# Attention with hashed buckets into a gated feed-forward layer: one pair of heads is loaded, turned around and hashed in another way

## The chip, the cores and the metric

The kernel runs on one core of a Trainium2 chip. The metric is the device time of one execution in microseconds (us). The time before is a median of 336.03 us over three runs, from 335.37 to 336.10 us.

## The reference, cut to what matters

There are 4 batches of 8 heads, 768 positions and 64 features a head. A query may attend to a key only if both fall into the same bucket of 64, found by the signs of six projections.

```python
q_bits = (einsum('bhsd,dk->bhsk', q, proj) > 0)      # proj: 64 x 6
k_bits = (einsum('bhsd,dk->bhsk', k, proj) > 0)
mask   = q_bucket[..., :, None] == k_bucket[..., None, :]
scores = where(mask, q @ k.T / sqrt(64), -1e9)
attn   = softmax(scores)                              # + 1e-9 in the sum
x      = (attn @ v) as rows of 3072 x 512             # heads side by side
xn     = x / sqrt(mean(x * x) + 1e-6) * rms_g         # the norm
out    = (silu(xn @ w_gate) * (xn @ w_val)) @ w_out   # 512 -> 1536 -> 512
```

## The kernel before, in words

**Units, heads and steps.** The work is cut into eight units: unit `u` is half `u % 2` of the queries of batch `u // 2`, 384 queries by eight heads. A head of a unit is three steps, each of which makes the scores of 256 keys by 384 queries (two matmuls, `scores`, L322) and their exponentials (one ScalarE instruction, `probs`, L334). There are 192 such steps, 24 for a unit. The order of heads is (unit 0, heads 0 and 1), (unit 1, heads 0 and 1), then the rest of unit 0, the rest of unit 1, and units 2 to 7. Unit 0 thus ends its scores with step 29, and unit 2, the first of batch 1, begins with step 48.

**The plan.** At every step the program issues the scores of the next step, the exponentials of this one, and then all that is listed in `plan[t]`, in the order in which `at(0, t, ...)` entered it. Engines and DMA queues run their instructions in this order, so a list entry that waits holds back whatever comes behind it on its engine. The last thing of a head is `av` (L347), attention times V, in two parts; `attn_out` (L361 to L373) scales its result into `x` and squares it, and `sumsq` (L377) sums the squares.

**Pairs of heads.** Keys and queries of two heads come together, as the pair `(b, hp)`. A pair is loaded on SyncE's DMA queue (`load_natural`, L94, or `load_blocks`, L117, the latter in runs of 128 bytes), turned so that features lie on partitions, copied into the operand tile `QK` in 16 bits, and hashed: the six sign bits of each position become six more rows of `QK`, so that equal buckets give the highest score. Six pairs, all of batch 0 and the first two of batch 1, are turned by TensorE: `turn_pe` transposes three blocks of one head into a PSUM bank (L149), and VectorE copies it out (L151). These pairs are hashed by `hash_pairs` (L223: eight matmuls into two banks, on 64 rows each), `signs` (L212) twice, and `send` (L262: four DMAs of 9.0 KB). The ten other pairs are turned by VectorE and hashed by `hash_one` (L203: four matmuls into one bank, on 128 rows; `signs` once; L282: eight DMAs of 4.5 KB).

**The end of unit 0.** The steps around the change are 20 to 48. Unit 0's last head has its `av` in steps 30 and 31. In step 31 VectorE runs the last `attn_out` of the unit and the sums, GpSimd the power that gives `rstd` (L393); then `norm` multiplies two thirds of `x` (VectorE, L404), and in step 37 (`TX`) ScalarE the last third. Then `turn_x` transposes the normed rows (L411) into `xnT`. From step 38 on the first unit's `gate` and `value` matmuls (L428) are laid between the scores of unit 1 by `spread`, which holds a table of weights for each kind of work (`HASH` is 1000) and puts the hashes of `inserts` ahead of the first gate at or behind their step. The weights of the feed-forward layer come on GpSimd's DMA queue (`load_w`, L523), as six DMAs from step 22 on.

Of the kernel before, what the change touches and what calls it, by code (L numbers as in the profile page):

```python
# [8 lines left out]
FP32 = mybir.dt.float32  # L9
# [9 lines left out]
D = 64  # L19
# [3 lines left out]
HALF = 384  # L23
# [10 lines left out]
def kernel(  # L34
# [12 lines left out]
    nc = tc.nc  # L47
# [3 lines left out]
    lpool = ctx.enter_context(tc.tile_pool(name="lpool", bufs=8))  # L51
# [13 lines left out]
    ident = const.tile([128, 128], FP32, name="ident")  # L65
# [15 lines left out]
    def bank(name, shape=None, dt=FP32):  # L81
        return gps.tile(shape or [128, 512], dt, name=name, tag="g")


    raw = {}

    def load_natural(eng, b, hp, which, heads=(0, 1)):
# [10 lines left out]
            ),  # L98
        )

    def load_v(eng, b, hp):
        vn = lpool.tile([128, 2, 6, D], FP32, name="vn", tag="L")
        eng.dma_start(
            out=vn.rearrange("p h c d -> p h (c d)"),
            in_=v[b, 2 * hp : 2 * hp + 2].rearrange("h (p c) d -> p h (c d)", c=6),
        )
        raw[b, hp][2] = vn
# [18 lines left out]


    PARITY = (0, 1)
    ONPE = [(0, hp) for hp in range(4)] + [(1, 0), (1, 1)]
    KROWS = D + 6  # L130
    qT, kT, QK = {}, {}, {}

# [8 lines left out]
    def turn_pe(b, hp, hh, which, keep=nc.vector.tensor_copy, act=(), ps=None):  # L141

        src = raw[b, hp][0 if which == "q" else 1][:, hh].rearrange(
            "p (j e) d -> p j (e d)", e=2
        )
        if ps is None:
            ps = bank("t_ps", [128, 3, 128])
        for j in range(3):
            nc.tensor.transpose(ps[:, j, :], src[:, j], ident)  # L149
        psf = ps.rearrange("p j t -> p (j t)")  # L150
        keep(turned(b, hp, which)[:, hh, :], psf)  # L151
        o = 0 if which == "q" else S
        for e in act:
            nc.scalar.copy(
                QK[b, 2 * hp + hh, "h"][0:64, o + e * HALF : o + (e + 1) * HALF],
                psf[64 * e : 64 * e + 64, :],
            )

    def turned(b, hp, which):
        return (qT if which == "q" else kT)[b, hp].rearrange("p (h c) -> p h c", h=2)  # L160
# [26 lines left out]
    def cast_pool(b, hp, which):  # L187
        if (b, hp) in ONPE:
            for e in range(2):
                cast_part(b, hp, which, e)  # L190
            return
        src = (qT if which == "q" else kT)[b, hp]
        o = 0 if which == "q" else S
        for hh in range(2):
            nc.gpsimd.tensor_copy(  # L195
                QK[b, 2 * hp + hh, "h"][0:64, o : o + S], src[64 * hh : 64 * hh + 64, :]
            )
# [295 lines left out]
    load_natural(nc.sync, 0, 1, "k")  # L493
    load_natural(nc.sync, 0, 1, "q")
    load_v(nc.sync, 0, 0)
    load_v(nc.sync, 0, 1)
    load_natural(nc.sync, 0, 2, "k")
    load_natural(nc.sync, 0, 2, "q")
# [37 lines left out]
    def at(w, s, f, *a):  # L536
        plan[NS * w + s].append(lambda: f(*a))

    new_pair(0, 0)
    turn_pe(0, 0, 0, "k", act=(0,))  # L540
    spare = [
        scps.tile([128, 2, 512], FP32, name="s_ps")[:, 0, 0:HALF].rearrange("p (j t) -> p j t", j=3)
        for _ in range(2)
    ]
    turn_pe(0, 0, 0, "q", act=(0,), ps=spare[0])
    cast_part(0, 0, "k", 1, 0, 1)
    turn_pe(0, 0, 1, "k", ps=spare[1])
    idle(1)
    _, direct, _, _ = hash_direct(0, 0, (0,))
# [55 lines left out]
    at(0, 1, load_natural, nc.sync, 0, 3, "k")  # L605
    at(0, 1, load_natural, nc.sync, 0, 3, "q")
    at(0, 2, load_v, nc.sync, 0, 2)
    at(0, 2, load_v, nc.sync, 0, 3)
    at(0, 6, v_prep, 0, 1)
    at(0, 15, v_prep, 0, 2)  # L610
    at(0, 19, v_prep, 0, 3, nc.vector)
    for hp, t in enumerate((4, 16, 21, 31)):
        at(0, t, v_mean, 0, hp, 2, range(6))
    for i, t in enumerate((22, 34)):
        cols = slice(i * DFF // 2, (i + 1) * DFF // 2)
        at(0, t, load_w, wg, moe_w_gate, 0, 4, cols)
        at(0, t + 3, load_w, wv, moe_w_val, 0, 4, cols)
        at(0, 39 + 3 * i, load_w, wo, moe_w_out, 6 * i, 6)


    for hp, ts in ((0, (8, 22, 23, 24, 25, 24, 26, 26, 28, 42)), (1, (20, 27, 28, 29, 30, 29, 41, 32, 33, 43))):
        tl, ts = ts[0], ts[1:]
        for w in "kq":
            at(0, tl, load_natural, nc.sync, 1, hp, w)
        at(0, tl, load_v, nc.sync, 1, hp)
        at(0, ts[0], new_pair, 1, hp)
        for t, hh, w in zip(ts[0:4], (0, 1, 0, 1), "kkqq"):
            at(0, t, turn_pe, 1, hp, hh, w)
        at(0, ts[4], cast_pool, 1, hp, "k")
        at(0, ts[5], cast_pool, 1, hp, "q")  # L630
        if hp == 0:
            at(0, ts[6], hash_pair, 1, hp)
            at(0, ts[7], send_pair, 1, hp)
        at(0, ts[8], v_prep, 1, hp)
        at(0, ts[8], v_sum, 1, hp)

    spots = {
# [11 lines left out]
    TX = 37  # L649
# [9 lines left out]
    for n, (u, h) in enumerate(order):  # L659
        t = 3 * n + 4 - ((u, h) == (0, H - 1))  # L660
        for part in range(2):
            at(0, t + part, av, u, h, part)
        if h % 2:
            if (u, h) == (0, H - 1):

                at(0, t + 1, o_step, u, h // 2, nc.vector)
                at(0, t + 1, s_step, u, h // 2)
                at(0, t + 1, norm_scale, u)
                at(0, t + 2, hash_only, 1, 1)
                at(0, t + 2, hash_signs, 1, 1)  # L670
                at(0, t + 2, norm, u)
                at(0, TX, norm_third, u, 2, nc.scalar.mul)
                at(0, TX + 1, send_pair, 1, 1)
                at(0, TX - 1, idle, 2, bank)
                at(0, TX, idle, 1, bank)
                for c in range(3):
                    at(0, TX, turn_x, u, c, c == 2)
                continue
            at(0, t + 1, o_step, u, h // 2)
            at(0, t + (6 if h < 7 else 3), s_step, u, h // 2)  # L680
# [36 lines left out]
    for u in range(7):  # L717
# [11 lines left out]
        for i in range(9):  # L729
            c, n = divmod(i, 3)  # L730
# [12 lines left out]
    def behind_norm(t):  # L743

        return t - t % NS + 7 if 1 <= t % NS < 7 else t

    for (b, hp), (load, kturns, qturns, _) in spots.items():
        at(0, load, load_blocks, nc.sync, b, hp)
        at(0, load, load_v, nc.sync, b, hp)
        at(0, kturns[0], new_pair, b, hp)  # L750
        for w, turns in (("k", kturns), ("q", qturns)):
            for i, t in enumerate(turns):
                at(0, t, turn_dve, b, hp, w, i, len(turns))
            at(0, behind_norm(turns[-1] + 1), cast_pool, b, hp, w)
        t = behind_norm(qturns[-1] + 2)
        at(0, t, v_prep, b, hp)
        at(0, t, v_sum, b, hp)
# [64 lines left out]
```

## Time and profile before

| what | value |
|---|---|
| three runs | 335.37, 336.03, 336.10 us |
| profiled execution | 335.25 us, of which the traced span is 333.4 us |
| TensorE matmul | 325.7 us busy, 3004 instructions |
| VectorE | 238.0 us busy, 487 instructions |
| ScalarE | 225.3 us busy, 327 instructions |
| GpSimd | 152.9 us busy, 205 instructions |
| SyncE's DMA queue | 75528 packets, 25.45 MB |
| GpSimd's DMA queue | 3680 packets, 4.72 MB |

The page of the profile lists busy time by engine, the chain of work that ended last, and groups of instructions by line with their mean duration. The chain and the order of instructions can also be asked for any stretch of the span, in microseconds from its start, and so can the packets that the DMA queues moved in it.

### The profile page before, as it was taken

To read this page: it belongs to the slowest core of one execution; us is meant where nothing else is said; L and a number is where in the kernel's file an instruction comes from. 1 tells how busy PE (TensorE), PEld (TensorE's weight loads), DVE (VectorE), ACT (ScalarE), POOL (GpSimd) and SP (SyncE) were. 2 spreads that over 40 slices of the span, in tenths; PEclk is the share of its full clock that TensorE was granted. 3 is DMA by queue.
4 is the path that set the end of the run, shared out by engine and by line. 5 is a ranking of instruction groups with operands and counts; after the bars stand their busy time and mean duration, and the time that the engine had idled before them with its cause. 6 is when DMAs were issued, how large, how long until landed. Compare 5 with 4: busy or idle time off the path is not lost.

```text
span 333.4 us, 7810 instructions
## 1 busy us (share of the span) xinstructions
PE 325.7 (98%) x3004; PEld 196.8 (59%) x3004; DVE 238.0 (71%) x487; ACT 225.3 (68%) x327; POOL 152.9 (46%) x205
## 2 busy tenths in 40 slices
PE   7999989999999999999999999999999999999996
PEld 3576656655565565655566565655656566664554
DVE  3887877778878668876888568886776456674870
ACT  3899886676677667676767667776676857754322
POOL 3698859229724743726483622656371111122000
DMA  7941999978129545341807036001000010002002
GB/s 216 349 151 42 252 166 209 204 131 189 68 41 161 96 131 107 51 98 67 168 16 142 11 102 131 7 3 67 34 4 2 4 62 33 0 2 84 14 0 94
DMA packets 79692, 30.92 MB, mean 93 GB/s; under 512 B 64988, under 2 KB 76712, under 8 KB 79656
## 3 DMA queue, kind: packets, MB, share of 16 engines
q1 hardware_dynamic: 75528, 25.45, 32.4%
q0 software_dynamic: 3680, 4.72, 8.4%
q8 instruction: 23, 0.38, 0.5%
q10 hardware_dynamic: 448, 0.27, 0.3%
q14 instruction: 13, 0.11, 0.1%
HBM read 28.32 MB, written 6.29 MB: 104 GB/s over the span
## 4 chain that ended last, share of the span: by engine, by line
PE 86%; DVE 5%; DMA 3%; SPq 1%; POOL 1%; ACT 1%; issue 1%; ACTq 0%; DVEq 0%; POOLq 0%
PE v_ps L428 18%; PE g_ps L428 17%; PE s_ps L322 17%; PE y_ps L457 16%; PE o_ps L347 10%; PE d_ps L203 2%; PE t_ps L149 2%; PE x_ps L411 2%; PE d_ps L223 2%; DMA qL<-in_q_dram 2%; SPq L282 1%; DMA pj<-in_proj_dram 1%; DVE xn L404 1%; ACT psb L334 1%; PE y_ps L476 1%
## 5 line engine op out<-in xcount | busy, mean ns | idle before, releaser
L334 ACT ACTIVATE psb<-s_ps,ebias 128x768 f16<-128x768 f32 x192 | 167.9, 900 | 21.8 <-PE s_ps L322 20.8
L322 PE MATMUL s_ps<-QK 70*128 70x384 f16 x384 | 93.6, 326 | 1.9 <-ACT psb L334 1.5
L436 ACT ACTIVATE t<-g_ps 128x384 f32<-128x384 f32 x96 | 47.2, 492 | 54.5 <-PE g_ps L428 54.3
L428 PE MATMUL g_ps<-xnT,wg 128*128 128x384 f16 x384 | 82.6, 325 | 0.1
L428 PE MATMUL v_ps<-xnT,wv 128*128 128x384 f16 x384 | 81.7, 325 | 0.2 <-DVE a L445 0.2
L445 DVE SCALAR_TENSOR_TENSOR a<-t,g_ps 128x384 f32<-128x384 f32 x96 | 52.8, 550 | 27.5 <-ACT t L436 25.9
L368 POOL TENSOR_TENSOR x<-otmp,rcp 128x384 f32<-128x384 f32 x31 | 25.9, 837 | 96.0 <-DVE rcp L366 95.5
L457 PE MATMUL y_ps<-wo,ht 128*128 128x512 f16 x276 | 68.0, 378 | 0.0
L347 PEld LDWEIGHTS <-psb 128*128 128x128 f16 x1152 | 52.0, 97 | 16.0 <-issue 1.2
L446 DVE SCALAR_TENSOR_TENSOR ht<-a,v_ps 128x384 f16<-128x384 f32 x96 | 53.2, 554 | 11.4 <-PE v_ps L428 3.2
L347 PE MATMUL o_ps<-vl,psb 128*128 128x65 f16 x1152 | 56.3, 193 | 0.0
L322 PEld LDWEIGHTS <-QK 70*128 70x128 f16 x384 | 34.6, 98 | 35.6 <-issue 12.7
L428 PEld LDWEIGHTS <-wv 128*128 128x128 f16 x384 | 35.2, 97 | 22.3 <-issue 1.4
L428 PEld LDWEIGHTS <-wg 128*128 128x128 f16 x384 | 34.7, 97 | 21.1 <-DVE xnT L417 0.6
L457 PEld LDWEIGHTS <-ht 128*128 128x128 f16 x276 | 24.6, 97 | 22.6
L373 POOL TENSOR_TENSOR sq<-x 128x384 f32<-128x384 f32 x31 | 25.7, 827 | 2.4
L469 ACT COPY ysb<-y_ps 128x512 f32<-128x512 f32 x23 | 13.5, 586 | 19.6 <-PE y_ps L457 19.6
L195 POOL CAST QK<-qT 64x768 f16<-64x768 f32 x20 | 16.6, 832 | 19.0 <-DVE qT L182 17.0
L361 DVE TENSOR_TENSOR otmp<-o_ps,cvb 128x390 f32<-128x390 f32 x32 | 17.8, 557 | 8.7 <-PE o_ps L347 8.5
L377 DVE TENSOR_REDUCE ssp<-sq 128x3 f32<-128x384 f32 x32 | 16.9, 529 | 9.9 <-POOL sq L373 9.7
L195 POOL CAST QK<-kT 64x768 f16<-64x768 f32 x20 | 16.5, 826 | 12.6 <-PE s_ps L322 7.3
L404 DVE TENSOR_SCALAR xn<-x,rstd 128x512 f16<-128x512 f32 x23 | 16.1, 754 | 7.2 <-POOL rstd L393 7.2
(79 smaller groups left out, 263.6 us busy)
## 6 DMA issues: line engine op xcount, KB each, us to landing
vn<-in_v_dram SPq DMA_DIRECT2D x16, 384.0 KB
out_dram<-ysb SPq DMA_DIRECT2D x23, 256.0 KB
qL<-in_q_dram SPq DMA_DIRECT2D x40, 96.0 KB
kL<-in_k_dram SPq DMA_DIRECT2D x40, 96.0 KB
kn<-in_k_dram SPq DMA_DIRECT2D x5, 384.0 KB
qn<-in_q_dram SPq DMA_DIRECT2D x5, 384.0 KB
wg<-in_moe_w_gate_dram POOLq DMA_DIRECT2D x2, 768.0 KB, 8.2
wv<-in_moe_w_val_dram POOLq DMA_DIRECT2D x2, 768.0 KB, 10.4
```

The source lines that it names most:

```text
L195: nc.gpsimd.tensor_copy(QK[b, 2 * hp + hh, "h"][0:64, o : o + S], src[64 * hh : 64 * hh + 64, :])
L322: nc.tensor.matmul(ps[:, j, 0:HALF], QK[b, h, "h"][0:KROWS, S + jt * 128 : S + (jt + 1) * 128], QK[b, h, "h"][0:KROWS, half * HALF : (half ...
L334: nc.scalar.activation(psb[u, h][:, 2 * ch : 2 * ch + 2, :], sps.pop((u, i))[:, :, 0:HALF], AF.Exp, bias=ebias, scale=ESCALE,)
L347: nc.tensor.matmul(o[:, c, hh, 0:65], psb[u, h][:, jt, c * 128 : (c + 1) * 128], vls[b % 2][:, h, 2 * (jt % 3) + jt // 3 if b in PARITY el ...
L368: eng.tensor_mul(xd.rearrange("p c (h d) -> p c h d", h=2), tmp[:, :, :, 0:64], r.to_broadcast([128, 3, 2, 64]),)
L373: eng.tensor_mul(sq, xd, xd)
L404: mul(xn[u][:, c, :], x[u][:, c, :], rstds[u][:, c : c + 1])
L428: nc.tensor.matmul(ps, w[:, kt, fs], xnT[u][:, kt, :], start=(kt == 0), stop=(kt == 3))
L436: nc.scalar.activation(t, fbank[u, ft, "g_ps"], AF.Tanh, scale=0.5)
L445: nc.vector.scalar_tensor_tensor(out=a, in0=t, scalar=1.0, in1=g, op0=ALU.add, op1=ALU.mult)
L446: nc.vector.scalar_tensor_tensor(out=ht[u][:, ft, :], in0=a, scalar=0.5, in1=vv, op0=ALU.mult, op1=ALU.mult)
L457: nc.tensor.matmul(y, ht[u][:, ft, c * 128 : (c + 1) * 128], wo[:, ft, :], start=(ft == 0), stop=(ft == NF - 1),)
```

## The change

Of the second pair of batch 1, `(1, 1)`, both tiles are now loaded by `load_mixed`, which lays the two heads side by side for every position: four DMAs instead of two, in runs of 64 numbers (256 bytes) instead of 384. A transposed block then holds both heads' features on 128 partitions, so that the pair can be hashed as `hash_one` does it. It is still turned by TensorE, twelve blocks by three (`turn_mixed`): the keys in steps 28 and 30 (four turns in steps 27 to 30 before), the queries in steps 32 and 33, between the sums of unit 0's norm and its multiplications. The hash in step 32 and its four sends in step 38 go; `hash_one` comes among unit 0's gates at step 42. The three matmuls on zeros in steps 36 and 37 are dropped. Some steps move: `v_mean` of pair (0, 3) from 31 to 29, the first weight loads from 22 and 25 to 21 and 24, the queries' cast of pair (1, 0) from 26 to 31, the casts of pair (1, 1) from 29 and 41 to 38 and 39.

```diff
+    def load_mixed(eng, b, hp):
+        tiles = []
+        for name, t in (("kn", k), ("qn", q)):
+            lt = lpool.tile([128, 6, 2, D], FP32, name=name, tag="L")
+            for hh in range(2):
+                eng.dma_start(
+                    out=lt[:, :, hh], in_=t[b, 2 * hp + hh].rearrange("(p c) d -> p c d", c=6)
+                )
+            tiles.append(lt)
+        raw[b, hp] = tiles[::-1] + [None]
...
-    ONPE = [(0, hp) for hp in range(4)] + [(1, 0), (1, 1)]
+    ONPE = [(0, hp) for hp in range(4)] + [(1, 0)]
...
+    def turn_mixed(b, hp, which, e, keep):
+        src = raw[b, hp][0 if which == "q" else 1]
+        ps = bank("t_ps", [128, 3, 128])
+        for j in range(3):
+            nc.tensor.transpose(
+                ps[:, j, :], src[:, 2 * j + e].rearrange("p h d -> p (h d)"), ident
+            )
+        dst = (qT if which == "q" else kT)[b, hp][:, e * HALF : (e + 1) * HALF]
+        keep(dst, ps.rearrange("p j t -> p (j t)"))
...
-    for hp, t in enumerate((4, 16, 21, 31)):
+    for hp, t in enumerate((4, 16, 21, 29)):
         at(0, t, v_mean, 0, hp, 2, range(6))
-    for i, t in enumerate((22, 34)):
+    for i, t in enumerate((21, 34)):
...
+    at(0, 31, cast_pool, 1, 0, "q")
...
+    at(0, 20, load_mixed, nc.sync, 1, 1)
+    at(0, 20, load_v, nc.sync, 1, 1)
+    at(0, 28, new_pair, 1, 1)
+    for e, t in enumerate((28, 30)):
+        at(0, t, turn_mixed, 1, 1, "k", e, nc.vector.tensor_copy)
+    at(0, 38, cast_pool, 1, 1, "k")
+    at(0, 39, cast_pool, 1, 1, "q")
...
     spots = {
+        (1, 1): (None, None, None, 42),
...
-                at(0, t + 2, hash_only, 1, 1)
-                at(0, t + 2, hash_signs, 1, 1)
-                at(0, t + 2, norm, u)
+                at(0, t + 2, turn_mixed, 1, 1, "q", 0, nc.vector.tensor_copy)
+                at(0, t + 3, turn_mixed, 1, 1, "q", 1, nc.vector.tensor_copy)
+                at(0, t + 3, norm, u)
                 at(0, TX, norm_third, u, 2, nc.scalar.mul)
-                at(0, TX + 1, send_pair, 1, 1)
-                at(0, TX - 1, idle, 2, bank)
-                at(0, TX, idle, 1, bank)
```

More of the change, by code (lines that the diff above doesn't have):

```diff
@@ L618 @@
         at(0, 39 + 3 * i, load_w, wo, moe_w_out, 6 * i, 6)
[L621 to L635, printed above, removed]
+    for w in "kq":
+        at(0, 8, load_natural, nc.sync, 1, 0, w)
+    at(0, 8, load_v, nc.sync, 1, 0)
+    at(0, 22, new_pair, 1, 0)
+    for t, hh, w in zip((22, 23, 24, 25), (0, 1, 0, 1), "kkqq"):
+        at(0, t, turn_pe, 1, 0, hh, w)
+    at(0, 24, cast_pool, 1, 0, "k")
+    at(0, 31, cast_pool, 1, 0, "q")
+    at(0, 26, hash_pair, 1, 0)
+    at(0, 28, send_pair, 1, 0)
+    at(0, 42, v_prep, 1, 0)
+    at(0, 42, v_sum, 1, 0)
+    at(0, 20, load_mixed, nc.sync, 1, 1)
[5 more added lines that the diff above has]
+    at(0, 39, cast_pool, 1, 1, "q")
+    at(0, 43, v_prep, 1, 1)
+    at(0, 43, v_sum, 1, 1)
     spots = {
[1 row of a table added]
         (1, 2): (34, (48, 48), (49, 49), 51),
@@ L747 @@
     for (b, hp), (load, kturns, qturns, _) in spots.items():
+        if load is None:
+            continue
         at(0, load, load_blocks, nc.sync, b, hp)
```

## The prediction

> **What bounds the kernel now.** I read the page first, then the chain of waits around the change in order of time, then the DMA queues by stretch, then SyncE's queue. The page:
>
> ```profile
> PE 325.7 (98%) x3004; PEld 196.8 (59%) x3004; DVE 238.0 (71%) x487; ACT 225.3 (68%) x327; POOL 152.9 (46%) x205
> ...
> PE 86%; DVE 5%; DMA 3%; SPq 1%; POOL 1%; ACT 1%; issue 1%; ACTq 0%; DVEq 0%; POOLq 0%
> ```
>
> TensorE carries 86% of the chain, so a matmul added there is paid, and so is any wait of TensorE, which runs in order. The exception matters here. The chain from 35 to 47 us (start, duration, what):
>
> ```profile
> 38.81 0.33 PE s_ps L322 x2
> 39.14 0.37 PE m_ps L307 x6
> ...
> 40.20 0.57 DVE otmp L361
> ...
> 42.81 0.18 DVE ss L389
> ...
> 43.04 0.44 issue
> 43.48 0.91 POOL rstd L393
> ...
> 44.41 1.05 DVE xn L404 x2
> ...
> 45.51 0.62 PE x_ps L411 x8
> ```
>
> From 39.5 to 45.5 us unit 0's norm is the bound. TensorE only keeps ScalarE's exponentials fed; in the chain its next pieces are the transposes, and the first gate starts at 47.00 us. So the hash (40.02 to 40.9 us) and the zeros (43.4 to 44.6 us) that the change takes away lie beside the norm.
>
> The DMA queues, each row giving packets, MB and share of 16 engines. First 32.5 to 35.4 us, where pair (1, 1) lands in packets of 1536 bytes:
>
> ```profile
> q1 hardware_dynamic: 711, 1.04, 99.4%
> ```
>
> Then 36 to 42 us, the weights (q0) over SyncE's queue (q1):
>
> ```profile
> q0 software_dynamic: 765, 1.15, 110.8%
> q1 hardware_dynamic: 43, 0.04, 2.5%
> ```
>
> Then 47 to 54 us, where pair (1, 2) in 128-byte packets meets more weights:
>
> ```profile
> q0 software_dynamic: 867, 1.31, 106.9%
> q1 hardware_dynamic: 864, 0.11, 19.8%
> ```
>
> Weights move at about 127 packets a us whether alone or in company; SyncE's queue, with both waiting, gets one packet for each of theirs, however small. Last, SyncE's queue, behind pair (1, 2):
>
> ```profile
> 62.29 2.95 SPq L262 DMA_DIRECT2D QK<-bits  x4
> 65.34 0.64 SPq L117 DMA_DIRECT2D qL<-in_q_dram  x1
> ```
>
> It issues without a pause worth the name from 62 to 86.5 us, about 0.7 us a DMA.
>
> **The change part by part.**
>
> *The norm starts earlier.* Steps 27 to 31 lose two turns before unit 0's last `av` (each three transposes, 0.33 us in the chain: 0.66 us); the limit becomes the exponentials, 0.79 us apart. Counting scores, turns, `v_mean` and `av` through, the last `av` ends near 39.3 us instead of 39.77, VectorE no longer has the `cvb` of `v_mean` (0.29 us) in front of `otmp`, and GpSimd, rid of 1.72 us of casts ahead of `x` and `sq`, gives the earlier sums sooner. `otmp` starts at 39.35 instead of 40.20: gain 0.85 us. Exponential 37, which ScalarE's third of the norm follows, goes from 43.73 to 42.95. By itself this brings the first gate to about 46.2: a gain of 0.8 us. The 0.44 us ahead of `rstd` occurs once (for later units the power starts 0.08 us after the sum ends), while the hash's two `signs` run on VectorE; if they cause it, up to 0.4 us more. I take none, since `rstd`'s first use explains it as well.
>
> *Turns, signs, zeros.* Twelve transposes and four copies stay. One `signs` (0.55 us of VectorE) goes. Zeros: 3 x 0.22 us at their pace, where TensorE waits anyway: nothing. The queries' two copies (1.1 us) sit between the sum and `xn` on VectorE, beside the power's 0.91 us plus the wait before it, as the two `signs` did: nothing, if the queries are there.
>
> *The hash among the gates.* Four matmuls on 128 rows are 0.78 us in the chain (eight on 64 rows 0.88), now in a stretch that is TensorE without a gap (15.00 busy of 47 to 62 us): +0.78 us. Its copy of signs hides beside VectorE's 11.04 of those 15 us.
>
> *The load.* This decides. Before, the pair comes as 512 packets; now as 2 x 1536 of 256 bytes. One costs, on the line between 128 bytes (12.9 ns, from 2084 packets at 84.2% in 67 to 69 us) and 1536 bytes (64.9 ns, from the row above), about 17.6 ns: 909 a us, an estimate from rows. Issues start at 30.88 us as before, packets flow at about 32.5. The weights' first DMA is issued from 32.07 to 33.08 us; one step earlier in the plan changes nothing, since GpSimd has no work between the two places. The next DMA passes the casts of the keys, and follows at 33.9 instead of 35.99: no gap in the weights. Before, their first packet came at 35.4, 2.3 us after the issue, when the 1536-byte ones ran out; a later one (issue ending at 45.2) took 0.75 us, small packets ahead. The 1.6 us between are some 25 packets of 65 ns already queued. With 17.6 ns ones that is 0.45 us, so the weights join at about 34.3. By then (34.3 - 32.5) x 909 = 1640 packets are through: the keys, in time for their turn at 35.8, and 100 of the queries. The other 1430 are 90 to an engine. The weights' 1024 are 64 to an engine and take 8.0 us; meanwhile the queries get 64, the remaining 26 take 0.5 us: landed at 42.8, seen by TensorE at about 43.2. If the weights join at 35.4 as before, 27 to an engine are left, and the queries are seen at 39.2. If each packet costs the 25.7 ns of the mixed stretch from the start, 44.2. I take 43.2: the short queue ahead is the nearer case.
>
> *Who waits.* The queries' turn in step 32 is due at 39.45. Behind it on TensorE stand the scores of step 34 on, so ScalarE runs dry at 40.7. With queries at 43.2: exponential 34 at 44.1, then 0.79 us each, 37 at 46.45; ScalarE's third ends at 48.0 instead of 45.26, the transposes about 48.4 instead of 46.13, first gate 49.2 instead of 47.00: +2.2 us. `xn` on VectorE waits behind both copies, to 45.7: earlier than ScalarE's third. The sum is 2.2 + 0.78 = +3.0 us. Each us of the queries' arrival moves the gates by one: at 39.2 they come 0.8 earlier (sum 0), at 41.5 they come 0.5 later (+1.3), at 44.2 they come 3.2 later (+4.0).
>
> *SyncE's queue.* Eight sends for four add 4 x 0.70 = 2.8 us behind 62.3 us. The loads behind them are wanted 3 us later or more. The tight one is pair (1, 2)'s hash: its sends start at 80.71, the second lands at 83.7, and the scores that need it start at 85.02. A 2.8 us shift less up to 0.9 us of pauses makes them 0.6 to 1.5 us late, unless TensorE is itself 3 us later: nothing in my main case, a rival otherwise. The first read of the moved hash is step 53, at 73.2: the eight sends end near 68. Casts of (1, 1) on GpSimd, at steps 38 and 39, come after `rstd`, and nobody needs them before step 48: nothing.
>
> The profiled execution took 335.25 us (span 333.4, 1.85 around it), 0.78 under the median. Its sum is 338.2; I add the 3.0 to the median: 339.0 us, own range 337.3 to 340.0 (the +1.3 and +4.0).
>
> **The rivals.**
>
> *The queries come in time and nothing else is late (not slower).* It holds if they are seen by about 40.3 us, when TensorE's wait just eats the gain of 0.8. For it: the weights' first packet waited until SyncE's queue was drained. Against it: the equal counts of 47 to 54 us. Then -0.8 + 0.78, less up to 0.4 for `rstd` and up to all of the hash if it fits a gap: 334.8 to 336.0, likeliest 335.6.
>
> *In time, but the sends are late.* Then 0.6 to 1.5 us at step 59, less up to 0.4: 336.3 to 337.5. For it: 1.3 us of slack against 2.8. Against it: pauses in the queue.
>
> *The clock falls.* The first eight zeros in this trace, at 1.2 to 4.1 us, took up to 634 ns, those at 43 us 377 to 380. A TensorE idle from 39.8 to 43.2, with no zeros behind, could lose that state, though the windows grant 1.00 throughout and no idle stretch after the start is over 0.76 us. Half pace for some 4 us, in a stretch where TensorE has 0.6 of each 0.79 us step, costs about 1.7 us more: 340.7. The Trainium skill (TensorE: Matmul & The Clock Gate, What's actually happening) states half the clock after an idle window of about 3.4 us; no run here shows it in mid-kernel.
>
> *The load is no different* (the program merges its runs) can't be: each head's 64 numbers lie between the other's.
>
> **How the numbers follow.** Late queries 0.52, clock 0.10, late sends 0.13, in time 0.25. Late queries and the clock are slower; of late sends 0.10 is slower by over 0.2% (0.67 us, about what a measurement of this kernel can tell from no change), 0.03 within; of in time 0.13 is faster by that, 0.12 within. Slower 0.72, same 0.15, faster 0.13. The range leaves out the better half of the faster cases and the worst of the clock: 335.2 to 340.6.
>
> **What would show it.** Right: 256-byte packets on SyncE's queue one for one with the weights from about 34 to 42 us; the first transposes of `turn_mixed` that read `qn` beginning near 43 us, with TensorE idle before it and ScalarE idle after exponential 33; first gate near 49; four `d_ps` of `hash_one` (0.78 us) more; 88 sends of 4.5 KB for 80. Wrong: queries turned by 39.5 us, a first gate at or before 46.5, or an idle TensorE ahead of the scores at 85 us instead.

## The result

The changed kernel takes 343.81 us (median of four runs, 343.51 to 345.84) against 335.96 us for the kernel before in the same comparison: a ratio of 1.0242 with a 95% interval of 1.0213 to 1.0270. That is 7.9 us slower. The prediction had the direction and the mechanism, but only 3.0 us of it, and the time lies outside its range.

The page of the changed kernel: busy time by engine, the granted TensorE clock in 40 slices of the span, and the chain that ended last.

```profile
PE 327.8 (96%) x2993; PEld 198.2 (58%) x2993; DVE 236.8 (69%) x486; ACT 225.4 (66%) x327; POOL 152.8 (45%) x205
...
PEclk9999969999999999999999999999999999999999
...
PE 82%; DMA 8%; DVE 5%; SPq 1%; ACT 1%; POOL 1%; issue 1%; ACTq 0%; POOLq 0%; DVEq 0%
```

TensorE has fewer instructions than before and more busy time, and one slice shows a lower clock: some matmuls ran slowly. DMA has gone from 3% of the chain to 8%. The chain in order of time names the transfer (start, duration, what):

```profile
33.12 13.29 DMA qn<-in_q_dram
46.42 0.14 issue
46.55 0.87 PE t_ps L176 x3
47.42 0.64 PE s_ps L345 x2
...
52.21 0.62 ACT xn L427
...
54.14 0.68 PE g_ps L451 x4
```

The queries' turn (L176) was due at 40.2 us, behind the scores of step 33, and starts at 46.55. Three transposes then take 0.87 us where 0.33 was the rule, and two score matmuls 0.64 instead of 0.33: half pace. The first gate starts at 54.14 us against 47.00 before. TensorE and the clock by stretch (length, then busy time of PE, PEld, DVE, ACT and POOL, then the granted clock, DMA share and GB/s):

```profile
40.00:43.00 3.00, 0.33 (x3) 0.00 (x0) 2.69 (x7) 1.46 (x2) 0.73 (x1) 1.00 1.16 201
43.00:50.00 7.00, 3.45 (x21) 2.60 (x22) 1.81 (x4) 1.52 (x2) 4.14 (x5) 0.53 1.19 229
```

TensorE had 0.33 us of work from 40 to 43 us. From about 43 us the clock is halved, while it is still idle; it comes back at 50.

The packets, first in 32 to 34 us (SyncE's queue alone, q1):

```profile
q1 hardware_dynamic: 1227, 0.31, 68.1%
```

Then 34 to 36 us, where the weights (q0) join:

```profile
q0 software_dynamic: 116, 0.18, 87.6%
q1 hardware_dynamic: 381, 0.09, 22.6%
```

And 36 to 43 us:

```profile
q0 software_dynamic: 788, 1.19, 93.0%
q1 hardware_dynamic: 752, 0.19, 20.7%
```

Alone, 1227 packets, nearly all of 256 bytes, take 68.1% of 2 us on 16 engines, 17.8 ns each. From 36 us on it is one for one, 752 to 788, and the queries crawl at 107 packets a us.

### The profile page after: what moved, and what is told of

It reads as the page before. It is cut to its first block, busy times and chain, and to the rows that moved or that the text cites. A ratio compares the mean times of both kernels' runs of the same rounds, so it can differ in the third digit from the quotient of the medians.

```text
span 341.8 us, 7795 instructions
## 1 busy us (share of the span) xinstructions
PE 327.8 (96%) x2993; PEld 198.2 (58%) x2993; DVE 236.8 (69%) x486; ACT 225.4 (66%) x327; POOL 152.8 (45%) x205
## 4 chain that ended last, share of the span: by engine, by line
PE 82%; DMA 8%; DVE 5%; SPq 1%; ACT 1%; POOL 1%; issue 1%; ACTq 0%; POOLq 0%; DVEq 0%
PE v_ps L451 17%; PE g_ps L451 17%; PE s_ps L345 16%; PE y_ps L480 15%; PE o_ps L370 9%; DMA qn<-in_q_dram 4%; PE d_ps L226 2%; PE x_ps L434 1%; SPq L305 1%; PE d_ps L246 1%; PE t_ps L161 1%; DMA pj<-in_proj_dram 1%; ACT psb L357 1%; DVE xn L427 1%; DMA kL<-in_k_dram 1%; PE y_ps L499 1%
## 5 line engine op out<-in xcount | busy, mean ns | idle before, releaser
L345 PE MATMUL s_ps<-QK 70*128 70x384 f16 x384 | 94.6, 329 | 2.1 <-ACT psb L357 1.6
L370 PEld LDWEIGHTS <-psb 128*128 128x128 f16 x1152 | 52.4, 97 | 16.8 <-issue 2.1
L218 POOL CAST QK<-qT 64x768 f16<-64x768 f32 x22 | 18.3, 830 | 19.0 <-DVE qT L205 17.0
L218 POOL CAST QK<-kT 64x768 f16<-64x768 f32 x22 | 18.2, 826 | 13.0 <-PE s_ps L345 7.6
```

The costliest lines, as they stand in the source:

```text
L218: nc.gpsimd.tensor_copy(QK[b, 2 * hp + hh, "h"][0:64, o : o + S], src[64 * hh : 64 * hh + 64, :])
L345: nc.tensor.matmul(ps[:, j, 0:HALF], QK[b, h, "h"][0:KROWS, S + jt * 128 : S + (jt + 1) * 128], QK[b, h, "h"][0:KROWS, half * HALF : (half ...
L370: nc.tensor.matmul(o[:, c, hh, 0:65], psb[u, h][:, jt, c * 128 : (c + 1) * 128], vls[b % 2][:, h, 2 * (jt % 3) + jt // 3 if b in PARITY el ...
```

## The experiments

**Small packets alone.** The kernel before, with nothing but the load cut:

```diff
+        if (b, hp) == (1, 1):
+            for e in range(2):
+                src = (q, k)[i][b, 2 * hp : 2 * hp + 2].rearrange("h (p j e) d -> e p h j d", e=2, j=3)
+                dst = raw[b, hp][i].rearrange("p h (j e) d -> e p h j d", e=2)
+                for hh in range(2):
+                    eng.dma_start(out=dst[e][:, hh], in_=src[e][:, hh])
+            return
```

> The kernel before, with only the key and query loads of pair (1, 1) cut into runs of 256 bytes (four DMAs a tensor, the same 3072 packets as in the change, layout, turns and hash as before). Theory: the load alone does it; the queries' turn, due at 37.1 us, waits to about 46 us and the norm behind it too: first gate 53 to 56 us, time 342.5 to 345.5 us. Rival (the load is harmless, the moved work costs the time): 335.5 to 336.7 us.

Measured: 347.08 us, ratio 1.0337 (1.0312 to 1.0362). That is 11.2 us, more than the whole change and more than I expected. TensorE's rows, with its wait and what ended it in brackets ("issue" where the profile shows nothing):

```profile
40.05 0.88 PE L156 MATMUL t_ps<-ident,kn 128*128 128x128 f32 x3 [4.23 <-issue]
...
43.54 0.87 PE L156 MATMUL t_ps<-ident,kn 128*128 128x128 f32 x3 [1.97 <-issue]
...
46.61 0.87 PE L156 MATMUL t_ps<-ident,qn 128*128 128x128 f32 x3 [1.07 <-DMA qn<-in_q_dram]
```

So the small packets alone, with the weights' DMAs in their old places, make TensorE wait, and the queries come at the same 46.6 us. But this is not the change's load. It has four DMAs for each tensor where the change has two, and issues them until 39.8 us, where the change is done at 33.8. From 32 to 35 us SyncE's queue moved 805 packets, against 1559 in the changed kernel, and the keys alone are 1536. So here the keys were most probably late too: of the 7.3 us of waiting, 6.2 stand ahead of the keys' turns. All these turns stand ahead of unit 0's last head and of its norm, and the clock is halved from 38.7 to 52.4 us. The 11.2 us are thus no price of the change's load, and whether turning the queries inside the norm made that load cheaper isn't shown.

**Zeros in the wait.** The changed kernel with one line more:

```diff
+                at(0, t + 2, idle, 28, bank)
                 at(0, t + 2, turn_mixed, 1, 1, "q", 0, nc.vector.tensor_copy)
```

> The changed kernel with 28 matmuls on zeros (128x512, 0.215 us each, 6.0 us) ahead of the queries' turn in step 32, so that TensorE is busy while it would wait. Theory (the wait costs some 5.5 us and the lost clock some 1.7 us on top): clock 1.00 throughout, the turn still starts at 46 to 46.6 us but at full pace, first gate at 52.2 to 52.8 us, time 341.7 to 342.5 us. Rival (the slow clock costs nothing, since ScalarE's exponentials set the pace there): 343.4 to 344.2 us.

Measured: 342.30 us (342.06 to 342.52), 1.5 us less than the changed kernel; clock 1.00. Its TensorE in order of time:

```profile
40.06 6.21 PE L541 MATMUL z_ps<-zeros 128*128 128x512 f16 x28
47.02 0.52 PE L176 MATMUL t_ps<-ident,qn 128*128 128x128 f32 x3 [0.76 <-DMA qn<-in_q_dram]
```

and its first gate in the chain:

```profile
53.12 0.68 PE g_ps L451 x4
```

The turn comes 0.47 us later than in the changed kernel, the gate 1.0 us earlier. So the lost clock costs some 1.5 us, and the wait is there whatever TensorE does meanwhile.

**Weights later.** The changed kernel with its first two weight loads at steps 25 and 26:

```diff
-    for i, t in enumerate((21, 34)):
+    for i, t in enumerate((25, 34)):
...
-        at(0, t + 3, load_w, wv, moe_w_val, 0, 4, cols)
+        at(0, t + (1 if i == 0 else 3), load_w, wv, moe_w_val, 0, 4, cols)
```

> The changed kernel with the first two weight loads at steps 25 and 26 instead of 21 and 24, nothing else. Theory (the 256-byte packets share the engines one for one with the weights, so the queries come 6 us late, and the idle TensorE loses its clock on top): the weights' first packets come at about 36 us, when pair (1, 1) is through; the queries' turn starts by 40.2 us, no TensorE idle over 1 us, clock 1.00, first gate at 46.3 to 47.5 us, time 335.5 to 337.5 us. Rival (the hash among the gates, the turns inside the norm and the eight sends cost the time): 341 us or more, with the queries early.

Measured: 341.21 us, ratio 1.0154 (1.0124 to 1.0183): only 2.6 us better. Half of the expectation held. The queries' turn starts at 40.50 us, no idle TensorE, clock 1.00, first gate near 47.1. The time of the profiled execution went into two other waits. In its chain, the second weights now come late:

```profile
36.51 12.18 DMA wv<-in_moe_w_val_dram
48.69 0.05 issue
48.74 0.82 PE v_ps L451 x4
```

And at step 60, in TensorE's timeline, the scores wait for the bits of pair (1, 2):

```profile
89.44 0.48 PE L345 MATMUL s_ps<-QK 70*128 70x384 f16 x2 [2.12 <-DMA QK<-bits]
```

That is the rival of the late sends, at a higher price than its 0.6 to 1.5 us. In the changed kernel it stays hidden, since TensorE is 8 us late by then. The profiled execution, at 339.90 us with a clock of 1.00, is the fastest of the four; the others took 341.18 to 342.10 with a mean clock of 0.995. Some of their time is thus probably clock lost in such a wait, which no trace shows.

**Load earlier.** The whole mixed load at step 17:

```diff
-    at(0, 20, load_mixed, nc.sync, 1, 1)
+    at(0, 17, load_mixed, nc.sync, 1, 1)
```

> The changed kernel with the mixed load at step 17 instead of 20 (V stays at 20), ahead of the sends of pair (0, 3). Theory (the packets only have to be through before the weights start at 34 us): issues from about 25.7 to 28.3 us, landed by 31 us, the queries' turn starts by 40.2 us, clock 1.00; the sends of pair (0, 3) go out some 0.3 us later, which the scores of step 24 see; time 335.5 to 337.5 us. Rival (it is the moved hash and turns): 341 us or more.

Measured: 337.59 us, ratio 1.0057 (1.0037 to 1.0078). With the same packets, ahead of the weights, 6.2 us are back. The turn starts at 42.15 us without waiting for its data. What is left shows in the chain: the sends of pair (0, 3), now behind the load, come late for step 24.

```profile
30.36 3.10 DMA QK<-bits
33.60 0.48 PE s_ps L345 x2
```

**Queries early, keys in place.** To spare those sends, only the queries are loaded at step 17:

```diff
+    at(0, 17, load_mixed, nc.sync, 1, 1, "q")
+    at(0, 20, load_mixed, nc.sync, 1, 1, "k")
```

> The changed kernel with the mixed queries loaded at step 17 and the mixed keys at step 20, so that neither runs into the weights and the sends of pair (0, 3) aren't held up. Theory (with the load in time, what is left are the hash among the gates, +0.6 us, and pair (1, 2)'s sends behind four more DMAs, seen as a TensorE wait at the scores of step 60, 2.3 us in the run with later weights): no wait at steps 24 and 34, first gate within 0.5 us of 47 us, a wait of 1.3 to 2.5 us at step 60, 337.0 to 338.5 us. Rival (the sends cost nothing and only the load matters): 335.5 to 336.5 us, no wait at step 60.

Measured: 337.34 us, ratio 1.0042 (1.0025 to 1.0059). The time is as expected, for another reason in the profiled execution. It shows no wait at step 60; instead the keys came late for step 28:

```profile
32.24 5.96 DMA kn<-in_k_dram
38.20 0.14 issue
38.34 0.52 PE t_ps L174 x3
```

That execution ran 0.6 us late from its start, and its last keys fell among the weights. The run with the zeros, below, ran 0.4 us late and had its keys in time, so what decided it isn't known, nor how often it happens in the unprofiled executions.

**Sends ahead of loads.** In addition the load of pair (2, 0) moves behind the hash of (1, 2):

```diff
-        (2, 0): (50, (63, 64, 65, 66), (67, 69, 70, 71), 73),
+        (2, 0): (52, (63, 64, 65, 66), (67, 69, 70, 71), 73),
```

> As the run before, and the load of pair (2, 0) at step 52 instead of 50, so that pair (1, 2)'s eight sends go ahead of its nine DMAs. Theory: the wait at step 60 goes, 1.3 to 2.5 us less than the run before, 335.5 to 336.7 us; equal to the kernel before within its uncertainty, since the norm's earlier start and the hash among the gates cancel. Rival (the wait at step 60 has another cause): as the run before.

Measured: 336.18 us, ratio 1.0014 (0.9998 to 1.0029): equal to the kernel before, 1.2 us less than the run ahead of it. SyncE's queue shows the new order, the sends from 75.62 us, then the load:

```profile
75.62 5.78 SPq L303 DMA_DIRECT2D QK<-bits  x8
81.50 2.71 SPq L127 DMA_DIRECT2D qL<-in_q_dram  x4
```

No TensorE wait for data is left in its profile between 24 and 100 us, neither for the keys nor for the bits. I can't divide the 1.2 us between the two, since the run ahead had the keys' wait in its profile. First gate in the chain:

```profile
46.33 0.68 PE g_ps L449 x4
```

**With the zeros.** The same with the three matmuls on zeros back.

```diff
+                at(0, TX - 1, idle, 2, bank)
+                at(0, TX, idle, 1, bank)
```

> As the run before, with the three matmuls on zeros of steps 36 and 37 back. Theory: TensorE waits there anyway, and without a wait of several us it keeps its clock with or without them: the same within 0.2 us. Rival (the zeros hold the clock up): 1 us or more faster, and the run before shows a stretch at half clock.

Measured: 336.30 us, ratio 1.0018 (0.9999 to 1.0036), the same as without them.

**Without the zeros, alone.** The kernel before with those two lines taken out.

> The kernel before with its three matmuls on zeros in steps 36 and 37 dropped, that part of the change alone. Theory: nothing, 335.7 to 336.3 us at a clock of 1.00. Rival (they hold the clock up): 337 us or more, with a stretch at half clock behind 44 us.

Measured: 336.10 us, ratio 1.0005 (0.9988 to 1.0023), clock 1.00 in the profiled execution. In the median the dropped zeros neither cost nor bring anything; what lost the clock in the changed kernel was a wait of 6 us. But in five of the twelve executions the mean clock was 0.995, while none of the 35 of the kernel before was under 0.999. These five average 336.80 us, the seven others 335.86. So the zeros may hold the clock up in some executions. That isn't shown: no trace shows where the clock was lost, and the run with sends ahead of loads, also without zeros, had no execution under 0.998.

**Long runs.** The changed order of work, with the load as before and two products for each transpose:

```diff
-            nc.tensor.transpose(
-                ps[:, j, :], src[:, 2 * j + e].rearrange("p h d -> p (h d)"), ident
-            )
+            for h in range(2):
+                nc.tensor.matmul(
+                    ps[64 * h : 64 * h + 64, j, :], src[:, h, 2 * j + e], ident,
+                    start=True, stop=True, tile_position=(0, 64 * h),
+                )
...
-    at(0, 20, load_mixed, nc.sync, 1, 1)
+    for w in "kq":
+        at(0, 20, load_natural, nc.sync, 1, 1, w)
```

> The changed kernel at the same steps, but pair (1, 1) loaded as before (two DMAs, runs of 1536 bytes, at step 20) and each block turned by two products of 64 columns with the identity instead of one transpose of 128, so that the heads still come to lie side by side. Theory (the size of the packets is the cause, not the order of work): the queries' turn starts by 41 us, no half clock, first gate by 49 us; the 24 products for 12 transposes cost TensorE 1.3 to 4 us beside the exponentials; with the wait at step 60 336.5 to 340 us. Rival (the order of turns and hash makes the wait): a TensorE wait for the queries of several us as in the changed kernel, 342 us or more.

Measured: 338.58 us, ratio 1.0085 (1.0050 to 1.0119); 5.2 us less than the changed kernel, at the same steps. From its chain, a queries' turn (its six products are listed twice), and the next scores directly behind it:

```profile
41.38 0.81 PE t_ps L177 x12
42.18 0.43 PE s_ps L347 x2
```

The queries wait for nothing. Each turn takes 0.81 us instead of 0.33, which accounts for 1.9 us of TensorE over four turns, partly hidden. Its profiled execution, the slowest of six at 341.87 us, also had the wait at step 60, 2.25 us up to 89.62, and behind it lost the clock for 3.4 us (columns as above):

```profile
86.50:89.90 3.40, 1.15 (x8) 0.52 (x6) 2.66 (x5) 1.28 (x2) 2.08 (x3) 1.00 0.40 125
89.90:93.30 3.40, 3.40 (x20) 1.86 (x18) 0.55 (x1) 1.27 (x2) 3.20 (x5) 0.50 0.03 7
```

The five others had a mean clock of 0.999 or 1.00.

**Moves alone.** The kernel before with `v_mean` at step 29 and the queries' cast of pair (1, 0) at 31.

> The kernel before with two of the change's moves alone: v_mean of pair (0, 3) in step 29 instead of 31, the queries' cast of pair (1, 0) in step 31 instead of 26; load, turns, hash and zeros as before. Theory (the norm's earlier start in the change comes in part from these): the last sum of unit 0 begins 0.3 us earlier, first gate 0.3 us earlier, 335.5 to 335.8 us. Rival (the two turns taken out of steps 27 to 30 are all of it): 335.9 to 336.1 us.

Measured: 335.91 us, ratio 0.9999 (0.9981 to 1.0018). The first gate is no earlier (46.94 us for its first matmul, 46.84 before). The expectation of 0.3 us failed, though not at the start: `otmp` begins at 39.99 us instead of 40.20. But the moved cast then runs on GpSimd from 40.31 to 42.23 us, and beside it VectorE's two products, `x` and `sq`, take 0.74 and 1.06 us, where they took 0.58 and 0.56. The sum of squares ends at 43.44 us instead of 42.99, and only because the power follows it sooner (last section) is the first gate not later still.

No version here beats the kernel before.

## Why the prediction was wrong

**The mechanism was right.** The weights joined at 34.1 us (estimated 34.3), a small packet alone took 17.8 ns (17.6), the keys were in time, the queries went one for one with the weights, and their turn waited with everything behind it on TensorE. Taking the weights away in time, the load ahead of them or the small packets out each removed the wait: three ways that agree.

**The term that was mis-sized is the queries' arrival.** I had 43.2 us; the turn started at 46.55. The weights' 1024 packets were given 8.0 us, at the 127 a us that held alone and nearly held (124) beside 128-byte packets. They took from 34.1 to 45.2 us, 11.1 us. Three parts of about 1 us each make the difference: 116 came in the two us in which they joined, where 127 a us makes 254; then 788 in seven, 113 a us; and the last 24 took 1.1 us. The kernel before has such an end too: with little beside them the same 1024 took 9.3 us (35.4 to 44.7). The 8.0 us left it out. The last queries landed 0.6 us behind the weights. My upper end for it, 44.2, priced only the small packets higher and kept the weights' pace fixed; the pace was not bounded at all. By the prediction's own rule, a us of gate for a us of arrival, a turn at 47.02 puts the gate at 53.0, and the run with zeros had just this turn and its gate at 53.12; 46.55 gives 52.5, and the clock makes it 54.14.

**The clock was a rival at 0.10, and came.** Priced at 1.7 us, measured at 1.5. The two errors are one: the longer wait brought the clock with it. The rule of the Trainium skill that stood there (TensorE: Matmul & The Clock Gate, What's actually happening: half clock after an idle window of about 3.4 us) agrees with this trace: the last scores at full pace end at 40.3 us, and the stretch from 43 to 50 us has a clock of 0.53. As a lower bound it fails in the profiled execution of the long runs, where a wait of 2.25 us was followed by half clock; the 2.12 us of later weights left it at 1.00. The measurement decides, and 0.10 for a wait of 3.4 us was probably too low.

**The hash among the gates** was +0.78 us. In the run without late data (sends ahead of loads), the steps are 0.67 us early at the first gate and 0.45 us late by step 72: 1.1 us for the matmuls and what the re-spread gates lose. The early norm was 0.8 us of gain in the sum and 0.67 there, which is close by luck: the sum of squares ended 0.74 us earlier, the power followed it 0.34 us sooner, which the prediction did not count, and the multiplications (`xn`) took 1.45 us instead of 1.04, which it did not count either. The rival in which queries come in time was thus right in kind; it forecast 335.6 us, at most 336.0, and the run has 336.18.

**SyncE's queue.** The four more sends cost nothing in the changed kernel, as the main case said, and 2.1 and 2.25 us of waiting at step 60 in two runs where the queries come in time (later weights, long runs).

**`rstd`.** I put the 0.44 us ahead of it down to a first use. That is refuted: the power is as much a first use in the runs that start it 0.15 us after the sum. That the signs did it, the other reading, isn't shown either (last section).

The sum as measured, on the profiled executions (333.4 and 341.8 us of span): first gate 7.1 us later (2.2 in the prediction), of which about 1.5 are the clock and the rest the wait less the early norm; then 1.15 us of hash and re-spreading by step 72 (0.78 in the prediction); the remaining 0.1 comes behind the last exponential.

## What to carry to other kernels

A load that is cut into smaller runs is not priced by its bytes, nor by its packets alone: here it got one packet for each of the weights' (752 to 788), so ask which transfers it will meet, and load it before them. When a wait is estimated from a shared rate, bound that rate too, with its start and its end; a rate that nearly held beside 128-byte packets (124 a us) did not hold beside 256-byte ones (113). A wait of TensorE must be priced with the clock that it may lose: here 6 us lost it, and once 2.25 us did.

## What the runs showed of the hardware that was not expected

**The wait ahead of GpSimd's power is neither a first use nor the signs alone.** The kernel before, from 42.6 us on: the sum of squares (L389) ends at 42.99 us, the hash's signs (L212) start on VectorE, and the power (L393) only at 43.48.

```profile
42.81 0.17 DVE L389 TENSOR_REDUCE ss<-ssp 128x3 f32<-128x15 f32 x1
43.02 1.02 DVE L212 TENSOR_SCALAR bits<-d_ps 128x384 uint16<-128x384 uint16 x2
...
43.48 0.90 POOL L393 TENSOR_TENSOR rstd<-ss,mhalf 128x3 f32<-128x3 f32 x1 [2.29 <-DVE ss L389]
```

The run with moves alone, with the same signs in the same place:

```profile
43.26 0.17 DVE L389 TENSOR_REDUCE ss<-ssp 128x3 f32<-128x15 f32 x1
...
43.47 1.02 DVE L212 TENSOR_SCALAR bits<-d_ps 128x384 uint16<-128x384 uint16 x2
...
43.59 0.90 POOL L393 TENSOR_TENSOR rstd<-ss,mhalf 128x3 f32<-128x3 f32 x1 [1.35 <-DVE ss L389]
```

From the end of the sum to the power it is 0.49 or 0.50 us in three kernels, all with the signs behind the sum (the kernel before, the one without zeros, small packets alone). It is 0.15 us in moves alone, and in the eight others, where copies of turned queries or nothing stand behind the sum. All are first uses, so it isn't that. The signs are there in each long wait, but also in one short one, so they don't make it by themselves. GpSimd had been idle for 1.35 us there and for 2.29 us or more in the three; whether that matters wasn't tried.

**Weights lose pace beside other packets, and start slowly.** In the middle they move at 113 packets a us beside 256-byte packets, against 127 alone. In the two us in which they join it is 58 a us, but more than the queries' packets must be at work: from 34.5 to 35.0 us both queues of the changed kernel nearly stand still.

```profile
q0 software_dynamic: 6, 0.01, 29.4%
q1 hardware_dynamic: 38, 0.01, 8.2%
```

With the load earlier, with few packets beside them, the weights begin slowly too: 58 from 35 to 36 us, against 98 in their first us before. What holds up the start wasn't tried.

**Half clock came in stretches of 3.4 us.** It lasted 3.4 us in the long runs (89.9 to 93.3 us), 6.8 us, twice that, in the changed kernel (43.4 to 50.2) and 13.7 us, four times that, with small packets alone (38.7 to 52.4).
